# A fold that adds once instead of twice, and mirror values taken from the even part from step 18 on, with an earlier plan for the first two batches

## The chip, the cores and the metric

One core of one Trainium2 chip. The time is device time in microseconds (us). The kernel before took a median of 675.4 us (three runs, 675.08 to 675.92). The experiments were run in five rounds each (four to six runs of each), beside eleven runs of the kernel before on the same chip.

## The reference

```python
def _attn_ref(x):                       # x: 8 x 3008 x 256
    X = np.fft.fft(x, axis=1)
    X = np.fft.fft(X, axis=2)
    return X.real.astype(np.float32)

def _moe_ref(x, w_gate, w_val, w_out):  # 24064 x 256, d_ff 1536
    gate = np.maximum(x @ w_gate, 0.0)
    val = x @ w_val
    return (gate * val @ w_out).astype(np.float32)
```

A real 2-D Fourier transform of every batch, then a gated FFN on its rows. Inputs and output are float32.

## The kernel before

The transform over s (3008 = 94 x 32) is done in two stages on TensorE; the one over d (256) is folded into the FFN weights. Because the input is real, output row s and the mirror row S-s come from the same two products: P (even) and Q (odd). So only half the rows are transformed, and each FFN step makes two tiles of h: one for the rows (gate G, value V) and one for the mirror rows (gate G - 2Q-part, value V - 2Q-part).

The work is 8 batches x 3 blocks x 12 slices of d_ff = 288 steps. A step does five or six matmuls of 512 (or 480) columns and eight of 256 columns for the output. Meanwhile GpSimd (called POOL in the profile) folds the x of a later batch: it adds and subtracts mirror rows, so that the transform over s needs half the rows.

The fold, in chunks of three rows (`XC = 3`):

```python
def fold(b, eng):
    xl, xh, eo = xt[b]
    for lo in range(1, J - 1, XC):
        ...
        yield eng.tensor_tensor(c1, x1, rev, op=ALU.subtract)     # 768 elements
        yield eng.tensor_tensor(x1, x1, rev, op=ALU.add)          # 768 elements
        yield eng.tensor_tensor(e1[:, :, H + 1:D], c1[:, :, 1:H], ..., op=ALU.subtract)   # 381
        eng.tensor_copy(...)                                      # 6
        yield eng.tensor_tensor(e1[:, :, 1:H], x1[:, :, 1:H], ..., op=ALU.add)            # 381
    ...
```

The mirror value is made in one of two ways. In an unsplit step TensorE adds a third matmul to V and VectorE multiplies. In a split step VectorE makes E, the even part (V after its first matmul plus the "nb" row), then 2E - V, and POOL multiplies; one matmul is saved:

```python
def split(t):
    return NBLK * NF + 8 <= t < len(steps) and t % 3 != 2        # from step 44

def mirror_value(t):
    if split(t):
        nc.vector.scalar_tensor_tensor(E, E, 2.0, V, op0=ALU.mult, op1=ALU.subtract)
        mirror_h(t, nc.gpsimd, e["E"])
    else:
        nc.tensor.matmul(V, lhsT=wm[1]..., rhs=pq..., start=False, stop=True, ...)
        mirror_h(t, nc.vector, e["V"])
```

`nb` is one row of 512 numbers, spread over all partitions by way of DRAM. It is made at the end of stage 2 by two transfers, the second of which waits for the first:

```python
nc.sync.dma_start(out=row, in_=pq[0:1, 1, :])                                # Nd <- pq
nc.sync.dma_start(out=nbt[b, blk][:], in_=view(row, 0, [[0, 128], [1, 512]]))  # nb <- Nd
```

`gm` is the mirror gate after ReLU, in SBUF. "Rotate" is a small matmul that mends one column of the shuffled data before stage 2 reads it; VectorE casts its result back.

A table says at which step of batch b the parts for the next batches are placed: load of x (b+2), start of its fold, stage 1 (b+1), shuffle through DRAM, rotate, and six stage-2 pieces.

```python
plan = {0: (28, 34, (14, 16, 18, 19, 21, 23, 24, 25), 26, 33, (33, 34, 36, 38, 40, 42)),
        1: (12, 19, range(11, 19), 19, 26, (26, 27, 29, 31, 33, 35)),
        2: (7, 13, range(6, 14), 14, 22, (23, 25, 27, 29, 31, 33))}     # batches 2 to 7
```

`gm` and `E` are SBUF tiles with four buffers each (`ep = ...(name="ep", bufs=4, ...)`), V has three banks of PSUM.

## Time and profile before

| | before |
|---|---|
| median time | 675.4 us |
| TensorE (PE) busy | 643.4 us, 96% |
| VectorE (DVE), ScalarE (ACT), POOL busy | 74%, 64%, 64% |
| share of PE in the chain that ended last | 94% |
| steps 18 to 35 / batch 1 / each later batch | 42.24 / 79.42 / 76.33 us |

The last row is worked out from the timeline: a step is taken to begin where its second gate matmul begins, and the stretches are differences of such starts.

The page of the kernel before: busy time by engine, the chain that ended last by engine, and three groups of the fold (busy us, mean ns of one | idle before).

```profile
span 673.5 us, 12515 instructions
...
PE 643.4 (96%) x4218; PEld 419.9 (62%) x4297; DVE 500.8 (74%) x800; ACT 428.9 (64%) x811; POOL 428.5 (64%) x590
...
PE 94%; DMA 2%; DVE 2%; issue 1%; ACT 1%; SPq 0%; DVEq 0%; ACTq 0%
...
L99 POOL TENSOR_TENSOR xc<-xl,xh 94x768 f32<-94x768 f32 x35 | 63.6, 1817 | 39.6 <-DMA xl<-in_x_dram 24.8
L100 POOL TENSOR_TENSOR xl<-xl,xh 94x768 f32<-94x768 f32 x35 | 63.5, 1814 | 1.2
...
L104 POOL TENSOR_TENSOR eo<-xl 94x381 bf16<-94x381 f32 x35 | 34.8, 995 | 0.0
```

The fold is a large part of POOL's time, but the chain runs through PE. What is worth something is what shortens PE's stream or fills its gaps. The gaps are in the table of waits of PE (us in total, times, longest):

```profile
PE ps_169 L158 <- ACT w_98 L277: 12.0, 1, 12.0
PE ps_1264 L203 <- DVE t_1073 L192: 1.4, 1, 1.4
...
PE ps_2153 L203 <- DVE t_1949 L192: 1.1, 1, 1.1
```

The first is start-up. The two others are stage 2 of batches 1 and 2, which waits for the rotate result. The timeline of the kernel before (start us, us taken, engine, line, operation; in brackets the idle time before it and what ended it) shows how:

```profile
115.30 0.18 PE L191 MATMUL psr<-t_1073,rot 128*128 128x12 bf16 x1
...
115.50 0.65 DVE L475 TENSOR_TENSOR h<-gm,V 128x480 bf16<-128x480 f32 x1 [1.25 <-PE psr L191]
116.07 0.68 DVE L463 TENSOR_TENSOR h<-gs,V 128x512 bf16<-128x512 f32 x1
116.67 0.20 DVE L192 CAST t_1073<-psr 128x12 bf16<-128x12 f32 x1
116.93 0.38 PE L203 MATMUL ps_1264<-m_100,t_1073 128*128 128x128 bf16 x4 [1.44 <-DVE t_1073 L192]
```

The rotate matmul is at 115.30, its cast stands in VectorE's order behind two multiplies, and stage 2 stands right behind the rotate in PE's order (step 33 for both in the plan). So PE stands still for 1.44 us.

### The profile page before, as it was taken

The numbers are of one execution on the slowest core, as the hardware profiler recorded it, in microseconds if no ns is written. First come the engines' busy times: TensorE is split into PE (matmuls) and PEld (weight loads), VectorE is DVE, ScalarE is ACT, GpSimd is POOL, SyncE is SP. The second block draws the span as 40 slices with busy tenths as digits, with TensorE's granted clock in tenths as the row PEclk, the third lists the DMA queues.
The fourth block names the chain that finished last, engine by engine and source line by source line (L and its number), as shares of the span: only waits on it lengthen the run. The fifth ranks groups of instructions, "written<-read, shape, count | busy, mean of one in ns | idle before, by whom it ended". The sixth has DMA issues, their size and how long they took to land.

```text
span 673.5 us, 12515 instructions
## 1 busy us (share of the span) xinstructions
PE 643.4 (96%) x4218; PEld 419.9 (62%) x4297; DVE 500.8 (74%) x800; ACT 428.9 (64%) x811; POOL 428.5 (64%) x590
## 2 busy tenths in 40 slices
PE   2899999999999999999999999999999999999996
PEld 1444665666666666666666666666666666666665
DVE  8446555567787787887888888878878788888881
ACT  5455665667566757676666767676676766656562
POOL 1218910994999499946997399946997344344341
PEclk9999999999999999999999999999999999999999
DMA  9693138229413932277112931268211231211113
GB/s 240 209 224 47 43 97 236 63 52 216 147 48 90 231 97 57 60 158 212 47 45 66 228 119 41 77 142 212 57 46 51 69 107 39 79 33 46 46 33 92
DMA packets 31844, 70.75 MB, mean 105 GB/s; under 512 B 4410, under 2 KB 21426, under 8 KB 29394
## 3 DMA queue, kind: packets, MB, share of 16 engines
q1 hardware_dynamic: 29444, 58.16, 31.9%
q0 software_dynamic: 2336, 11.80, 8.7%
q8 instruction: 33, 0.54, 0.4%
q14 instruction: 31, 0.25, 0.1%
HBM read 39.77 MB, written 30.96 MB: 105 GB/s over the span
## 4 chain that ended last, share of the span: by engine, by line
PE 94%; DMA 2%; DVE 2%; issue 1%; ACT 1%; SPq 0%; DVEq 0%; ACTq 0%
PE po L505 38%; PE G L438 10%; PE V L461 9%; PE G L449 9%; PE V L459 8%; PE G L437 8%; PE V L487 4%; PE psw L251 4%; DMA xh<-in_x_dram 2%; DVE h L463 1%; DVE eo L130 0%; DVE E L469 0%; SPq L119 0%; ACT gm L452 0%; ACT os L508 0%
## 5 line engine op out<-in xcount | busy, mean ns | idle before, releaser
L505 PE MATMUL po<-wo,h 128*128 128x256 bf16 x2304 | 323.3, 273 | 1.8
L475 POOL TENSOR_TENSOR h<-gm,E 128x480 bf16<-128x480 f32 (+1 forms) x162 | 199.1, 1229 | 147.9 <-DVE E L483 147.2
L505 PEld LDWEIGHTS <-h 128*128 128x128 bf16 x2304 | 222.8, 98 | 82.7 <-issue 7.6
L452 ACT ACTIVATE gm<-G 128x480 f32<-128x480 f32 (+1 forms) x288 | 167.4, 581 | 134.0 <-PE G L449 130.4
L463 DVE TENSOR_TENSOR h<-gs,V 128x512 bf16<-128x512 f32 x288 | 190.6, 684 | 47.5 <-PE V L461 40.4
L439 ACT ACTIVATE gs<-G 128x512 f32<-128x512 f32 x288 | 171.8, 597 | 2.2 <-POOL si L399 2.2
L475 DVE TENSOR_TENSOR h<-gm,V 128x480 bf16<-128x480 f32 (+1 forms) x126 | 83.7, 664 | 87.8 <-ACT gm L452 63.2
L469 DVE SCALAR_TENSOR_TENSOR E<-nb,af,V 128x480 f32<-128x480 bf16 (+1 forms) x162 | 117.2, 723 | 7.4 <-PE V L459 5.9
L438 PE MATMUL G<-pq,ws_105 128*128 128x512 bf16 x287 | 108.8, 379 | 2.0
L449 PE MATMUL G<-pq,wm_107 128*128 128x480 bf16 (+1 forms) x288 | 106.7, 371 | 1.0 <-ACT gs L439 1.0
L483 DVE SCALAR_TENSOR_TENSOR E<-E,V 128x480 f32<-128x480 f32 (+1 forms) x162 | 106.6, 658 | 0.0
L461 PE MATMUL V<-pq,ws_106 128*128 128x512 bf16 x272 | 103.0, 379 | 0.2
L459 PE MATMUL V<-pq,wc_104 128*128 128x512 bf16 x265 | 100.5, 379 | 0.0
L508 ACT COPY os<-po 128x512 f32<-128x512 f32 x96 | 56.2, 585 | 68.3 <-PE po L505 68.3
L437 PE MATMUL G<-pq,wc_103 128*128 128x512 bf16 x249 | 94.4, 379 | 1.0 <-ACT pq L206 1.0
L99 POOL TENSOR_TENSOR xc<-xl,xh 94x768 f32<-94x768 f32 x35 | 63.6, 1817 | 39.6 <-DMA xl<-in_x_dram 24.8
L100 POOL TENSOR_TENSOR xl<-xl,xh 94x768 f32<-94x768 f32 x35 | 63.5, 1814 | 1.2
L461 PEld LDWEIGHTS <-ws_106 128*128 128x128 bf16 x288 | 28.2, 98 | 33.8 <-DVE ws_106 L256 0.4
L438 PEld LDWEIGHTS <-ws_105 128*128 128x128 bf16 x288 | 28.2, 98 | 32.4 <-issue 1.1
L487 PE MATMUL V<-pq,wm_108 128*128 128x480 bf16 (+1 forms) x126 | 46.6, 370 | 0.2
L459 PEld LDWEIGHTS <-wc_104 128*128 128x128 bf16 x288 | 28.2, 98 | 17.5 <-issue 1.3
L104 POOL TENSOR_TENSOR eo<-xl 94x381 bf16<-94x381 f32 x35 | 34.8, 995 | 0.0
(362 smaller groups left out, 401.5 us busy)
## 6 DMA issues: line engine op xcount, KB each, us to landing
out_dram<-os SPq DMA_DIRECT2D x176, 128.0 KB
xl<-in_x_dram SPq DMA_DIRECT2D x7, 1360.0 KB
nb<-Nd SPq DMA_DIRECT2D x24, 128.0 KB
xl<-in_x_dram SPq DMA_DIRECT2D x7, 238.0 KB
xl<-in_x_dram SPq DMA_DIRECT2D x2, 768.0 KB
xh<-in_x_dram SPq DMA_DIRECT2D x2, 768.0 KB
wst<-in_moe_w_gate_dram SPq DMA_DIRECT2D x6, 256.0 KB
wst<-in_moe_w_val_dram SPq DMA_DIRECT2D x6, 256.0 KB
```

Of the source, the lines that this page charges most:

```text
L437: nc.tensor.matmul(e["G"][:], lhsT=wc[0][:, fs], rhs=pq[:, 0, :], start=True, stop=False)
L438: nc.tensor.matmul(e["G"][:], lhsT=ws[0][:, fs], rhs=pq[:, 1, :], start=False, stop=True)
L439: nc.scalar.activation(e["gs"][:], e["G"][:], ACTF.Relu)
L449: nc.tensor.matmul(e["G"][:, cols], lhsT=wm[0][:, f * 128:(f + 1) * 128], rhs=pqt[b, blk][:, 1, cols], start=False, stop=True, skip_group_ ...
L452: nc.scalar.activation(e["gm"][:, cols], e["G"][:, cols], ACTF.Relu)
L459: nc.tensor.matmul(e["V"][:], lhsT=wc[1][:, fs], rhs=pq[:, 0, :], start=True, stop=split(t))
L461: nc.tensor.matmul(e["V"][:], lhsT=ws[1][:, fs], rhs=pq[:, 1, :], start=False, stop=True, skip_group_check=split(t))
L463: nc.vector.tensor_tensor(e["h"][:, 0, :], e["gs"][:], e["V"][:], op=ALU.mult)
L469: nc.vector.scalar_tensor_tensor(e["E"][:, cols], nbt[b, blk][:, cols], af[:, f:f + 1], e["V"][:, cols], op0=ALU.mult, op1=ALU.add)
L475: eng.tensor_tensor(free(e["h"][:], 512 + cols.start + NB - 1, [NB, (cols.stop - cols.start) // NB], [-1, NB]), e["gm"][:, cols].rearrange ...
L483: nc.vector.scalar_tensor_tensor(e["E"][:, cols], e["E"][:, cols], 2.0, e["V"][:, cols], op0=ALU.mult, op1=ALU.subtract)
L505: nc.tensor.matmul(po[:, s % 2, :], lhsT=ht[t - f + ff]["h"][:, sg, g * 128:(g + 1) * 128], rhs=wo[:, ff, :], start=(ff == 0), stop=(ff == ...
```

## The change

The intent: since x is folded over s and then over d, one add over s with d reversed, u[d] = x[s,d] + x[S-s,D-d], is enough; its even and odd parts over d are both results. That is one large operation on POOL per chunk instead of two, and fewer pieces (17 instead of 22 per fold). The room on POOL is used to split from step 18 on instead of 44, and batches 0 and 1 get an earlier plan.

```diff
     def fold(b, eng):
         xl, xh, eo = xt[b]
         for lo in range(1, J - 1, XC):
-            ...
-            yield eng.tensor_tensor(c1, x1, rev, op=ALU.subtract)
-            yield eng.tensor_tensor(x1, x1, rev, op=ALU.add)
-            yield eng.tensor_tensor(e1[:, :, H + 1:D], c1[:, :, 1:H], free(c1, D - 1, [D, n], [-1, H - 1]),
-                                    op=ALU.subtract)
-            eng.tensor_copy(free(e1, 0, [D, n], [H, 2]), free(x1, 0, [D, n], [H, 2]))
-            yield eng.tensor_tensor(e1[:, :, 1:H], x1[:, :, 1:H], free(x1, D - 1, [D, n], [-1, H - 1]), op=ALU.add)
+            n = min(XC, J - 1 - lo)
+            x1, e1, m = xl[0:NA, lo:lo + n, :], eo[:, lo:lo + n, :], (NB // 2 - lo) * D
+            eng.tensor_tensor(free(e1, 0, [D, n], [H, 2]), free(x1, 0, [D, n], [H, 2]),
+                              free(xh[0:NA], m, [-D, n], [H, 2]), op=ALU.add)
+            yield eng.tensor_tensor(x1[:, :, 1:D], x1[:, :, 1:D], free(xh[0:NA], m + D - 1, [-D, n], [-1, D - 1]),
+                                    op=ALU.add)
+            for op, o in ((ALU.add, 1), (ALU.subtract, H + 1)):
+                yield eng.tensor_tensor(e1[:, :, o:o + H - 1], x1[:, :, 1:H], free(x1, D - 1, [D, n], [-1, H - 1]),
+                                        op=op)
@@
-        return NBLK * NF + 8 <= t < len(steps) and t % 3 != 2
+        return 18 <= t < len(steps) and t % 3 != 2
@@
-    plan = {0: (28, 34, (14, 16, 18, 19, 21, 23, 24, 25), 26, 33, (33, 34, 36, 38, 40, 42)),
-            1: (12, 19, range(11, 19), 19, 26, (26, 27, 29, 31, 33, 35)),
-            2: (7, 13, range(6, 14), 14, 22, (23, 25, 27, 29, 31, 33))}
+    plan = {0: (18, 24, (16, 17, 18, 19, 20, 21, 22, 23), 24, 31, (32, 33, 35, 37, 39, 41)),
+            1: (7, 13, range(6, 14), 14, 22, (23, 25, 27, 29, 31, 33))}
@@
-        for k in range(2 if t < NBLK * NF + 8 else 1):
-            while folds and next(folds[0], folds) is folds:
-                folds.pop(0)
+        while folds and next(folds[0], folds) is folds:
+            folds.pop(0)
```

The last hunk is how fast a fold is handed to POOL: two pieces a step up to step 43 before, one piece a step now.

More of the change, by code (lines that the diff above doesn't have):

```diff
@@ L58 @@
     xp = ctx.enter_context(tc.tile_pool(name="xp", bufs=1, space=SB))
-    xcp = ctx.enter_context(tc.tile_pool(name="xcp", bufs=2, space=SB))
     tp = ctx.enter_context(tc.tile_pool(name="tp", bufs=2, space=SB))
@@ L93, in fold @@
         for lo in range(1, J - 1, XC):
-            hi = min(lo + XC, J - 1)
-            n = hi - lo
-            x1, e1 = xl[0:NA, lo:hi, :], eo[:, lo:hi, :]
-            rev = free(xh[0:NA], (NB // 2 - lo) * D, [-D, n], [1, D])
-            c1 = xcp.tile([NA, XC, D], F32, tag="xc", name="xc")[:, 0:n, :]
-            yield eng.tensor_tensor(c1, x1, rev, op=ALU.subtract)
-            yield eng.tensor_tensor(x1, x1, rev, op=ALU.add)
-            yield eng.tensor_tensor(e1[:, :, H + 1:D], c1[:, :, 1:H], free(c1, D - 1, [D, n], [-1, H - 1]),
-                                    op=ALU.subtract)
-            eng.tensor_copy(free(e1, 0, [D, n], [H, 2]), free(x1, 0, [D, n], [H, 2]))
-            yield eng.tensor_tensor(e1[:, :, 1:H], x1[:, :, 1:H], free(x1, D - 1, [D, n], [-1, H - 1]), op=ALU.add)
+            n = min(XC, J - 1 - lo)
[7 more added lines that the diff above has]
+                                        op=op)
         ends = free(xl[0:NA], 0, [(J - 1) * D, 2], [H, 2])
@@ L535 @@
     at(9, nyquist)
-    plan = {0: (28, 34, (14, 16, 18, 19, 21, 23, 24, 25), 26, 33, (33, 34, 36, 38, 40, 42)),
-            1: (12, 19, range(11, 19), 19, 26, (26, 27, 29, 31, 33, 35)),
-            2: (7, 13, range(6, 14), 14, 22, (23, 25, 27, 29, 31, 33))}
+    plan = {0: (18, 24, (16, 17, 18, 19, 20, 21, 22, 23), 24, 31, (32, 33, 35, 37, 39, 41)),
+            1: (7, 13, range(6, 14), 14, 22, (23, 25, 27, 29, 31, 33))}
     for b in range(B):
         t0 = b * NBLK * NF
-        tl, tf, t1, tsh, tr, t2 = plan[min(b, 2)]
+        tl, tf, t1, tsh, tr, t2 = plan[min(b, 1)]
         if b + 2 < B:
```

## The prediction

> **What bounds it now.** TensorE: the page has PE busy 643 of 673.5 us (96%), VectorE 74%, GpSimd (POOL) and ScalarE 64%; the chain of waits runs 94% through PE. The Trainium skill ("Perfetto Trace Analysis", Identifying the Most-Contended Engine) warns that matmul busy time is no measure of headroom, so I took PE's cadence from the timeline: 512 columns start every 0.213 us, back to back in nearly all steps. After start-up (34.8 us) the table of PE waits holds 1.44 and 1.11 us for the DVE cast of the "rotate" result (batches 1 and 2), and about 1 us once more. Where POOL is busy 33.98 of 34 us (238 to 272, 476 to 510), PE is still busy 33.79: POOL is not on the chain.
>
> **What the change does.**
> 1. Fold on POOL: a chunk becomes a 6-element add (0.21 us), one 765-element op (about 1.85, from the 768-element ones at 1.81) and two of 381 (0.99 each): 4.0 us, not 5.8; over 35 chunks 62 us less. Worth nothing by itself; it makes room for 2. Fold 1 should end near 73 us, not 82.
> 2. Split from step 18, not 44: 18 more steps get the mirror value from VectorE and POOL. Removed: 18 mirror matmuls, 0.20 to 0.21 us of PE cadence each. Added: 18 pairs of DVE ops (0.71 + 0.65) less 18 DVE multiplies (0.66), and 18 POOL multiplies (1.21 to 1.27). The skill's "GPSIMD Engine Reference" says GpSimd can't access PSUM; the trace agrees so far as every POOL multiply reads E, not V.
> 3. Plan: in batches 0 and 1 rotate and the first stage 2 now stand a step apart instead of in one step. From batch 2 on they already do, with no PE wait: the two waits go.
>
> **Sum, from step cadence** (starts of the second gate matmul).
> - Steps 18 to 35 take 42.24 us. In steady batches a triple of steps, two of them split, takes about 6.18 (512 columns) or 6.08 (480) without stage 1 or 2. After: 2 x 6.18 + 4 x 6.08, nine stage 1/2 groups at 0.215 and the rotate, about 38.75. Gain 3.5.
> - Batch 1 takes 79.42; a steady batch 76.33, plus three left-over stage-2 groups: 76.98. Gain 2.4.
> - Batches 2 to 7, start-up, tail: 0; only POOL gets slack.
>
> Total 5.9 us, all on the critical path: about 3.5 from matmuls left out, 2.4 from waits. Less 0.3 for small new stalls.
>
> **Prediction: 669.7 us, 8 in 10 between 668.2 and 672.0.** Faster by over 2%: 0.02; within 2%: 0.97; slower: 0.01.
>
> **What will show it.** 36 PE instructions fewer; mirror value matmul x108; POOL multiplies x180; POOL busy about 428 - 62 + 22 = 388 us; DVE up by about 12; no PE wait for the rotate cast; batch 1 near 77.0; batches 2 to 7 still 76.3 each; PE 95% of the chain.
>
> **What would make it wrong.** (a) Load x of batch 2 starts at step 18, its fold at step 24, some 13.4 us later; that load took 13.6 us before. If it lands late, in-order POOL holds the mirror multiplies behind the fold; gm has four buffers, so over about 4 us of lag reaches PE. (b) Splits at step 36 need the nb row made at step 33: two dependent transfers in some 6 us; a late one stalls VectorE, then PE through V's three banks. (c) The 765-element op with a fully reversed operand could be slower. (d) Eight stage 1 evacuations, one per step, load ScalarE to 2.0 of 2.2 us. Each could cost 1 to 2 us.

## The result, and the profile after

The changed kernel took a median of 669.73 us (four runs, 668.58 to 670.72) against 675.66. The ratio is 0.9912, 95% interval 0.9892 to 0.9932; repeated in five rounds it was 0.9901 (0.9888 to 0.9915). Ratios are the mean time of one kernel's runs over that of the other's runs of the same rounds, so they are not quite the ratio of the medians that are quoted.

The page of the changed kernel (its line numbers are two to four lower than before; L98 and L101 are the new fold, L473 the multiply on POOL):

```profile
span 668.5 us, 12493 instructions
...
PE 640.5 (96%) x4201; PEld 417.9 (63%) x4279; DVE 513.0 (77%) x818; ACT 428.7 (64%) x811; POOL 391.1 (59%) x573
...
PE 91%; issue 3%; DMA 2%; DVE 2%; POOL 1%; ACT 0%; SPq 0%; DVEq 0%; POOLq 0%
...
L473 POOL TENSOR_TENSOR h<-gm,E 128x480 bf16<-128x480 f32 (+1 forms) x180 | 221.0, 1228 | 208.4 <-DVE E L481 202.8
...
L101 POOL TENSOR_TENSOR eo<-xl 94x381 bf16<-94x381 f32 x70 | 68.7, 994 | 0.4
L98 POOL TENSOR_TENSOR xl<-xl,xh 94x765 f32<-94x765 f32 x35 | 63.2, 1805 | 2.7
```

There are 18 weight loads fewer (PEld x4297 to x4279), 18 VectorE instructions and 18 POOL multiplies more (x162 to x180), and POOL is busy 37 us less. The table of waits of PE no longer holds the two rotate waits; start-up and two short waits in the first steps (1.9 us; 1.0 in one before) are what is left of any size:

```profile
PE ps L156 <- ACT w L275: 12.1, 1, 12.1
PE G L447 <- ACT gs L437: 1.9, 2, 1.0
```

The timeline of the changed kernel at the same place shows the step put between rotate and stage 2 (the plan says 31 and 32):

```profile
109.86 0.18 PE L189 MATMUL psr<-t,rot 128*128 128x12 bf16 x1
...
110.13 0.69 DVE L461 TENSOR_TENSOR h<-gs,V 128x512 bf16<-128x512 f32 x1 [0.54 <-PE psr L189]
110.74 0.20 DVE L190 CAST t<-psr 128x12 bf16<-128x12 f32 x1
...
112.26 0.39 PE L201 MATMUL ps<-m,t 128*128 128x128 bf16 x4
```

The cast is done at 110.94, stage 2 comes at 112.26 without a wait.

Where the time went, by stretches of steps (starts of the second gate matmul, us, profiled runs):

| steps | before | after | difference |
|---|---|---|---|
| 0 to 11 | 31.98 | 32.87 | +0.89 |
| 12 to 17 | 13.72 | 13.73 | 0 |
| 18 to 35 | 42.24 | 38.59 | -3.65 |
| 36 to 71 (batch 1) | 79.42 | 77.28 | -2.14 |
| each of batches 2 to 6 | 76.33 | 76.33 | 0 |
| 252 to 286 | 71.40 | 71.23 | -0.17 |

The stretches are not the causes. Steps 18 to 35 hold only 12 of the 18 new splits, and they hold the first rotate wait (step 33); batch 1 holds the other six splits (steps 36 to 43) and the second wait. The profile of e6 below, the changed kernel without the early split, separates the two: it took 40.86 us in steps 18 to 35 and 27.30 in steps 36 to 47, where the changed kernel took 38.59 and 26.14. So the split is worth 2.27 us in the first stretch and 1.16 in the second, 3.43 in all, and 1.38 of the 3.65 us are the plan's.

The +0.89 in the first steps is not counted to the change: steps 0 to 11 took between 31.7 and 33.9 us in the fourteen profiles, with the new fold and without it. In the changed kernel's profile a copy on POOL (the one that releases the buffer of a weight load) waited 13.5 us for a weight load (12.2 before), and ScalarE's first gate output waited for that copy, 3.1 us instead of 2.2. This scatter is why a single run doesn't decide 1%.

### The profile page after: what moved, and what is told of

It is laid out like the page before. It is cut to its first block, busy times and chain, and to the rows that moved or that the text cites. A ratio compares the mean times of both kernels' runs of the same rounds, so it can differ in the third digit from the quotient of the medians.

```text
span 668.5 us, 12493 instructions
## 1 busy us (share of the span) xinstructions
PE 640.5 (96%) x4201; PEld 417.9 (63%) x4279; DVE 513.0 (77%) x818; ACT 428.7 (64%) x811; POOL 391.1 (59%) x573
## 4 chain that ended last, share of the span: by engine, by line
PE 91%; issue 3%; DMA 2%; DVE 2%; POOL 1%; ACT 0%; SPq 0%; DVEq 0%; POOLq 0%
PE po L503 38%; PE G L436 10%; PE V L459 10%; PE V L457 9%; PE G L447 9%; PE G L435 7%; PE V L485 3%; DMA xh<-in_x_dram 2%; PE psw L249 2%; PE ps L159 2%; PE ps L201 2%; DVE E L467 1%; DVE eo L128 0%; PE ps L164 0%; DVE h L461 0%
## 5 line engine op out<-in xcount | busy, mean ns | idle before, releaser
L473 POOL TENSOR_TENSOR h<-gm,E 128x480 bf16<-128x480 f32 (+1 forms) x180 | 221.0, 1228 | 208.4 <-DVE E L481 202.8
L473 DVE TENSOR_TENSOR h<-gm,V 128x480 bf16<-128x480 f32 (+1 forms) x108 | 71.9, 665 | 62.8 <-ACT gm L450 57.1
L436 PE MATMUL G<-pq,ws 128*128 128x512 bf16 x282 | 106.9, 379 | 2.6
L447 PE MATMUL G<-pq,wm 128*128 128x480 bf16 (+1 forms) x288 | 106.7, 370 | 1.9 <-ACT gs L437 1.9
L459 PE MATMUL V<-pq,ws 128*128 128x512 bf16 x280 | 106.0, 378 | 0.5
L457 PE MATMUL V<-pq,wc 128*128 128x512 bf16 x273 | 103.5, 379 | 0.0
L435 PE MATMUL G<-pq,wc 128*128 128x512 bf16 x239 | 90.6, 379 | 1.0 <-ACT pq L204 1.0
L101 POOL TENSOR_TENSOR eo<-xl 94x381 bf16<-94x381 f32 x70 | 68.7, 994 | 0.4
L98 POOL TENSOR_TENSOR xl<-xl,xh 94x765 f32<-94x765 f32 x35 | 63.2, 1805 | 2.7
L459 PEld LDWEIGHTS <-ws 128*128 128x128 bf16 x288 | 28.2, 98 | 34.0 <-DVE ws L254 0.4
L436 PEld LDWEIGHTS <-ws 128*128 128x128 bf16 x288 | 28.2, 98 | 32.4 <-issue 1.1
L169 ACT CAST t<-ps 96x512 bf16<-96x512 f32 x64 | 37.4, 584 | 6.3 <-PE ps L157 3.2
L485 PE MATMUL V<-pq,wm 128*128 128x480 bf16 (+1 forms) x108 | 40.0, 370 | 0.2
```

The lines of the kernel that those rows point to most:

```text
L435: nc.tensor.matmul(e["G"][:], lhsT=wc[0][:, fs], rhs=pq[:, 0, :], start=True, stop=False)
L436: nc.tensor.matmul(e["G"][:], lhsT=ws[0][:, fs], rhs=pq[:, 1, :], start=False, stop=True)
L447: nc.tensor.matmul(e["G"][:, cols], lhsT=wm[0][:, f * 128:(f + 1) * 128], rhs=pqt[b, blk][:, 1, cols], start=False, stop=True, skip_group_ ...
L457: nc.tensor.matmul(e["V"][:], lhsT=wc[1][:, fs], rhs=pq[:, 0, :], start=True, stop=split(t))
L459: nc.tensor.matmul(e["V"][:], lhsT=ws[1][:, fs], rhs=pq[:, 1, :], start=False, stop=True, skip_group_check=split(t))
L473: eng.tensor_tensor(free(e["h"][:], 512 + cols.start + NB - 1, [NB, (cols.stop - cols.start) // NB], [-1, NB]), e["gm"][:, cols].rearrange ...
```

## The experiments

The question was whether the sum of the prediction is right for the right reasons: is the gain the 18 matmuls and the two waits; is the fold worth nothing by itself, yet needed; and is the plan only about rotate? Each part was put into the kernel before alone, then each was taken out of the changed kernel alone. "Before" is the median of the kernel before in the same rounds: 676.15 us for e1 to e4, 675.84 for e5 to e8, 676.04 for e9 to e12; these three groups ran on three chips, so comparisons across groups, as of e7 with e9 and e10, lean on these medians agreeing to 0.3 us. All kernels gave correct results.

### e1: the fold alone

The kernel before with the new fold, handed over one piece a step.

```diff
-            yield eng.tensor_tensor(c1, x1, rev, op=ALU.subtract)
-            yield eng.tensor_tensor(x1, x1, rev, op=ALU.add)
+            (the new fold, as in the change)
-        for k in range(2 if t < NBLK * NF + 8 else 1):
```

> Only the cheaper fold (and its one piece per step) in the kernel before; split from step 44 and the old plan stay. Theory A (TensorE cadence and the rotate waits are all of the gain, the fold only makes room): POOL busy falls by about 60 us, from 428 to about 368, the time stays within 0.6 us of before, and the two rotate waits (1.4 and 1.1 us) stay in the table of PE waits. Rival B (POOL was holding the kernel back, its relief pays): 2 to 6 us faster.

676.09 us, ratio 0.9998 (0.9985 to 1.001). POOL busy fell from 428.5 to 370.1 us, and both rotate waits stayed (2.0 us in two). So 58 us of POOL are worth nothing by themselves, and rival B is out.

### e2: the plan alone

```diff
-    plan = {0: (28, 34, ...), 1: (12, 19, ...), 2: (7, 13, ...)}
+    plan = {0: (18, 24, ...), 1: (7, 13, ...)}
```

> Only the new plan (when batch 2 is loaded, when stage 1, shuffle, rotate and stage 2 run in batches 0 and 1); fold and split as before. Theory A: the two rotate waits go, 2.0 to 2.6 us faster, nothing else. Rival C (the whole gain is the matmuls left out by the split): within 0.6 us of before.

673.44 us, ratio 0.9959 (0.9947 to 0.9971): 2.7 us, a little over the expected range, and the rotate waits are gone.

### e3: rotate one step earlier, and nothing else

```diff
-    plan = {0: (28, 34, (14, 16, ...), 26, 33, (33, 34, ...)),
-            1: (12, 19, range(11, 19), 19, 26, (26, 27, ...)),
+    plan = {0: (28, 34, (14, 16, ...), 26, 32, (33, 34, ...)),
+            1: (12, 19, range(11, 19), 19, 25, (26, 27, ...)),
```

> The kernel before with two numbers changed: rotate in batch 0 at step 32 instead of 33 and in batch 1 at 25 instead of 26, so that it stands one step ahead of its first stage 2. Theory A: the same 2.0 to 2.6 us as the whole new plan gives, and no PE wait for the rotate cast. Rival D (the plan's gain comes from the earlier load and stage 1, not from rotate): under 0.6 us.

673.16 us, ratio 0.9953 (0.994 to 0.9965): 3.0 us by medians, as much as the whole plan within the intervals. In its profile steps 30 to 35 took 13.32 us instead of 14.92, steps 60 to 71 took 26.18 instead of 26.88; no wait for the rotate cast is left. Without the split, all that the plan gains is gained by two numbers in it.

### e4: the split alone

```diff
-        return NBLK * NF + 8 <= t < len(steps) and t % 3 != 2
+        return 18 <= t < len(steps) and t % 3 != 2
```

> Only the split from step 18; old fold (two pieces a step up to step 43), old plan. In steps 34 to 43 POOL is given about 30 us of fold and 9 us of mirror multiplies and memsets in some 21 us of TensorE time. Theory A (the fold makes room): the mirror multiplies fall behind, ScalarE waits for gm buffers, TensorE stalls by some 8 to 13 us there, so 4 to 10 us SLOWER than before although 18 matmuls are gone. Rival E (the cheaper fold was not needed): 3.0 to 3.7 us faster, as the sum of cadences says.

686.37 us, ratio 1.0146 (1.013 to 1.0162): 10 us slower, at the upper end of what was expected. Steps 18 to 35 gained 2.7 us (39.53 instead of 42.24), then steps 36 to 47 took 38.17 instead of 26.48. The timeline of e4 there:

```profile
138.67 1.82 POOL L99 TENSOR_TENSOR xc<-xl,xh 94x768 f32<-94x768 f32 x1
140.57 1.82 POOL L100 TENSOR_TENSOR xl<-xl,xh 94x768 f32<-94x768 f32 x1
...
144.50 1.20 POOL L475 TENSOR_TENSOR h<-gm,E 128x480 bf16<-128x480 f32 x1
...
145.73 0.57 ACT L452 ACTIVATE gm<-G 128x480 f32<-128x480 f32 x1 [3.09 <-POOL h L475]
...
146.84 0.36 PE L449 MATMUL G<-pq,wm 128*128 128x480 bf16 x1 [1.40 <-ACT gs L439]
```

This is the expected chain: a mirror multiply stands behind pieces of the fold, ScalarE can't write gm until that multiply has read its buffer, and PE waits for ScalarE. But the table of waits also held one that was not in the theory: PE waited 3.9 us once for an E of VectorE, and VectorE waited 4.2 us for nb.

### e5: the changed kernel without the new fold

```diff
+            (the old fold, as before)
-        while folds and next(folds[0], folds) is folds:
-            folds.pop(0)
+        for k in range(2 if t < 43 and t % 4 == 0 else 1):
+            while folds and next(folds[0], folds) is folds:
+                folds.pop(0)
```

> The changed kernel with the old fold put back. Its 22 pieces have to be done before the next load of x (step 43), as the new fold's 17 are, so up to step 42 every fourth step takes two pieces. Theory A (the fold only makes room, but the room is needed): from step 24 to 41 POOL has about 30 us of fold and 17 us of multiplies and memsets in some 38 us of TensorE time; about 5 us of lag were borne without a stall in the kernel before, so TensorE stalls by about 4 us: about 673.5, between 671.5 and 676. Rival E (the cheaper fold was not needed for the gain): as the changed kernel, 669 to 670.5.

678.91 us, ratio 1.0052 (1.0039 to 1.0064): 9 us slower than the changed kernel, twice what was expected, and slower than the kernel before. ScalarE waited 23.6 us for POOL's multiplies before it could write gm (3.8 in the changed kernel). The windows of e5 from 120 us on (busy us of each engine in 8 us; PE first, then weight loads, VectorE, ScalarE, POOL, then granted clock and DMA):

```profile
120.00:128.00 8.00, 7.43 (x56) 4.83 (x54) 5.83 (x10) 4.83 (x9) 8.00 (x11) 1.00 0.32 83
128.00:136.00 8.00, 6.96 (x47) 4.18 (x45) 5.31 (x9) 4.11 (x8) 8.00 (x11) 1.00 0.06 19
136.00:144.00 8.00, 6.96 (x47) 4.38 (x46) 4.88 (x9) 5.18 (x10) 8.00 (x13) 1.00 0.21 68
```

POOL is busy throughout, 8.00 of 8 us; PE is not. The same window of the changed kernel has PE back at its full 7.9 while POOL comes to rest:

```profile
128.00:136.00 8.00, 7.95 (x58) 5.41 (x57) 6.08 (x11) 5.93 (x12) 7.44 (x15) 1.00 0.06 19
136.00:144.00 8.00, 7.90 (x55) 5.51 (x56) 6.30 (x10) 5.85 (x12) 2.60 (x5) 1.00 0.95 248
```

The author reports that the old fold can't simply be handed over more slowly: the split alone with one piece a step and the old plan is said to deadlock when it is built, since 22 pieces from step 34 are not done when x is loaded again at step 48 (the arithmetic holds; the failed build is not on record). So at the rate of hand-over tried here the cheaper fold is needed: it turns a loss of 3 us into a gain of 6. Other rates for the old fold were not tried. How much lag POOL may have before PE feels it was estimated too high here.

### e6: the changed kernel without the early split

```diff
-        return 18 <= t < len(steps) and t % 3 != 2
+        return NBLK * NF + 8 <= t < len(steps) and t % 3 != 2
```

> The changed kernel with the split put back to step 44. Theory A: fold and plan together give what the plan alone gave, so 2.0 to 3.0 us faster than before, about 673.3; the 18 mirror matmuls of steps 18 to 43 are the rest. Rival B (POOL relief counts together with the plan): below 672.

673.41 us, ratio 0.9963 (0.995 to 0.9976): 2.4 us, what the plan gives alone. The split in steps 18 to 43 is the other 3.5 us, and by stretches 3.43, as said above.

### e7: the changed kernel without the new plan

```diff
-    plan = {0: (18, 24, ...), 1: (7, 13, ...)}
+    plan = {0: (28, 34, ...), 1: (12, 19, ...), 2: (7, 13, ...)}
```

> The changed kernel with the old plan (fold of batch 2 from step 34, rotate in the same step as its first stage 2). Theory A: fold and split together give 3.0 to 3.8 us, about 672.4; the two rotate waits of 1.1 to 1.5 us are in the table of PE waits; no stall from POOL, though the split alone cost 10 us, since the new fold asks 20 us of POOL in 17 steps and not 30 in 11. Rival: if the split alone was slow for another reason than POOL's load (VectorE, or early nb), this is slow too, over 676.

679.91 us, ratio 1.0057 (1.004 to 1.0075). This is a miss by 7.5 us: the kernel is slower than before, though POOL has the cheap fold. The expectation had named this outcome as the sign of another reason. The cause is at step 37. From the timeline of e7 (SPq is the queue that issues the transfers):

```profile
103.89 1.11 SPq L81 DMA_DIRECT2D xl<-in_x_dram  x2
103.97 1.02 POOL L84 DMA_INDIRECT xh<-in_x_dram,ix  x1 [0.17 <-issue]
...
119.14 0.23 SPq L210 DMA_DIRECT2D Nd<-pq  x1
125.74 0.34 SPq L211 DMA_DIRECT2D nb<-Nd  x1
...
128.81 0.71 DVE L467 SCALAR_TENSOR_TENSOR E<-nb,af,V 128x480 f32<-128x480 bf16 x1 [5.44 <-DMA nb<-Nd]
...
129.58 0.58 PE L459 MATMUL V<-pq,ws 128*128 128x512 bf16 x1 [5.21 <-DVE E L467]
```

The row of 1 KB was sent at 119.14, and the transfer that depends on it could be issued only at 125.74, 6.6 us later; in the kernel before the same pair was 1.15 us apart:

```profile
92.83 1.01 POOL L85 DMA_INDIRECT xh<-in_x_dram,ix  x1 [0.64 <-PE V L487]
...
105.62 1.11 SPq L82 DMA_DIRECT2D xl<-in_x_dram  x2
...
120.32 0.23 SPq L212 DMA_DIRECT2D Nd<-pq  x1
121.47 0.34 SPq L213 DMA_DIRECT2D nb<-Nd  x1
```

The load of x for batch 2 has two halves, xl issued by SPq and xh issued by POOL. In e7 they were issued together, at 103.89 and 103.97, and POOL's fold waited for xh until 125.12. In the kernel before POOL issued its half already at 92.83, 12.8 us ahead of the other, and the fold began at 119.18. That is an effect of the early split which the prediction did not have: the three runs with the old plan and the late split (before, e1, e3) issue xh at 92.8 to 94.0, and the three with the old plan and the early split (e4, e7, e8) at 102.8 to 104.0, where POOL's multiplies stand in front of it. So the split does two things to nb. Without it nobody needs this nb before step 44, and with it step 36 does; and it makes the load end later, so that the row is late. VectorE did nothing else for 5.4 us, and PE stood with it.

The wait cost more than its 5.2 us, since the clock fell. Windows of e7 around it (third number from the end of a line is the granted clock):

```profile
124.00:129.50 5.50, 0.37 (x2) 0.09 (x1) 0.69 (x1) 1.04 (x2) 4.30 (x7) 0.76 0.49 169
129.50:133.00 3.50, 3.42 (x13) 1.80 (x13) 1.99 (x4) 0.00 (x0) 0.96 (x3) 0.50 0.03 11
133.00:137.00 4.00, 4.00 (x29) 2.54 (x28) 2.31 (x4) 3.25 (x6) 3.92 (x5) 0.92 0.02 6
```

The clock record of the trace has 0.50 from 126.83 to 133.65. So 4.1 us of work after the gap ran at half clock, and 512 columns took 0.42 us to issue instead of 0.21. The Trainium skill ("TensorE: Matmul & The Clock Gate", Part 1: The HAM clock gate) says that after at least one idle window of about 3.4 us the array runs at half clock until it has been busy for about as long. The return agrees with this trace: PE was busy from 130.24 to 133.65, 3.41 us, before it. The fall came sooner: at 126.83 PE had been idle for 2.5 us, since 124.37. Steps 37 and 38 together took 11.67 us, against 4.38 in the changed kernel: 7.3 us more, of which 5.2 are the wait and about 2.0 the clock (an estimate, half of the 4.1 us).

### e8: the split alone, with six buffers instead of four for gm and E

```diff
-    ep = ctx.enter_context(tc.tile_pool(name="ep", bufs=4, space=SB))
+    ep = ctx.enter_context(tc.tile_pool(name="ep", bufs=6, space=SB))
```

> The split alone (10 us slower than before) with six buffers instead of four for gm and E. Theory A (the multiplies queue behind the fold on POOL, and the wait reaches TensorE through the gm and E buffers): two buffers more bear two steps more of lag, about 4.3 us, so 681 to 683 instead of 686.4, and steps 36 to 47 take about 34 us instead of 38.2. Rival F (the wait is for something else: the nb row, the h buffers, VectorE's own load): unchanged within 1 us.

684.76 us, ratio 1.0131 (1.0115 to 1.0148): 1.6 us better than e4, less than the 3.4 to 5.4 expected. In steps 36 to 47 the buffers did more than expected (32.25 us instead of 38.17), but steps 48 to 71 gave 3.9 us back (58.21 instead of 54.27). So the gm and E buffers do pass POOL's lag on to PE, and rival F is not all of it; but more buffers mostly put the wait off while POOL is overloaded. The wait for nb, 5.1 us at PE, stands in this profile too: F was right about part of e4's loss.

### e9: e7 with the load of x for batch 2 ten steps earlier

```diff
-    plan = {0: (28, 34, (14, 16, ...), 26, 33, (33, 34, ...)),
+    plan = {0: (18, 34, (14, 16, ...), 26, 33, (33, 34, ...)),
```

> The kernel without the new plan (679.9 us, when 672.4 was expected) with one number changed: x of batch 2 is loaded from step 18 instead of 28; fold, stage 1, rotate and stage 2 stay where the old plan has them. In its profile TensorE waited 5.2 us at step 37 for an E of VectorE, which waited 5.4 us for the nb row; the write of that row was issued at 119.1 us and landed only at 125.7, while the load of x was still under way. Theory G (the split needs nb at step 36, and the load of x holds the two small transfers up): the wait goes, 672 to 674 us; what is left to the changed kernel is the two rotate waits. Rival H (stage 2 one step later is the cause, two dependent transfers don't fit into two steps): 677 or more.

672.54 us, ratio 0.9949 (0.9937 to 0.9961). One number is worth 7.4 us. Rival H is out: stage 2 stands where it stood. In the timeline of e9 the first transfer now has the way free:

```profile
85.19 0.89 SPq L81 DMA_DIRECT2D xl<-in_x_dram  x2
...
117.98 0.23 SPq L210 DMA_DIRECT2D Nd<-pq  x1
119.12 0.34 SPq L211 DMA_DIRECT2D nb<-Nd  x1
```

1.14 us lie between the two, and no wait of VectorE for nb is left. What remains to the changed kernel, 2.7 us, is the rotate: PE waits for it twice in this profile, 1.7 us together. No run takes the delay of so small a transfer apart, but the packet records in the traces show what stood before it. In e7 the row's one packet of 1024 bytes started at 125.04. The packets of xl, issued before it on the same SPq queue, ended at 122.65, those of xh on POOL's queue at 124.40, and those of the output stores, issued at 108.41 on SPq, at 125.20. In the kernel before these ends were at 118.56, 101.71 and 119.82, and the row's packet started at 121.02, 0.7 us after its issue. So the row stood behind older transfers of its own queue; xl took 15.4 us from its first packet to the end of its last with xh beside it (e7), and 9.6 us without (before). The Trainium skill ("DMA: Bandwidth & Descriptors", Issuing engines are not separate DMA queues) says that transfers of all issuing engines run on the same 16 DMA engines and interleave; the 6.6 us of e7, with both halves under way, and the 1.14 us of e9, with none, fit that.

### e10, e11, e12: the changed kernel again, and a denser split

e11 uses the room that is left: three of four steps split from step 48 on, and the later folds spread out.

```diff
-        return 18 <= t < len(steps) and t % 3 != 2
+        return 18 <= t < len(steps) and (t % 3 != 2 if t < 48 else t % 4 != 3)
@@
-        while folds and next(folds[0], folds) is folds:
+        while (t < 49 or t % 3) and folds and next(folds[0], folds) is folds:
```

e12 has only the first of these two hunks. e10 is the changed kernel, unaltered.

> The changed kernel unaltered, for a narrow interval beside the others: 669 to 671 us, ratio 0.990 to 0.993.

> The changed kernel with three of four steps split from step 48 on instead of two of three (20 more mirror matmuls left out), and the folds from batch 3 on spread to two pieces in three steps (17 pieces in 25 steps, before the next load). Theory A (TensorE cadence decides as long as POOL and VectorE keep up; VectorE would be at about 7.5 of 8.0 us in four steps, POOL at about 1.9 of 2.0 us a step): 20 x 0.17 = 3.4 us faster than the changed kernel, 665.5 to 667.5. Rival I (three splits in a row exhaust V's three banks or VectorE): no gain or slower.

> As the one before, but the folds keep one piece a step. POOL is then asked for about 2.36 us a step during a fold, against some 2.03 of TensorE, over 17 steps: 5.6 us of lag, a little over the 4 to 5 that were borne. Theory A: up to 1.5 us of stall in each of batches 2 to 5, so 667 to 672, slower than the spread version. Rival J (the lag that is borne is larger): the same as the spread version.

| | median us | ratio to before (95%) |
|---|---|---|
| e10 changed kernel | 669.88 | 0.9901 (0.9888 to 0.9915) |
| e11 denser, folds spread | 663.24 | 0.9816 (0.9803 to 0.9828) |
| e12 denser, one piece a step | 664.91 | 0.9829 (0.9813 to 0.9845) |

e11 beats both kernels, and by twice what was expected: 6.6 us, which is 0.33 for each of its 20 extra splits, not 0.17. In the stretch without folds, steps 252 to 286, the changed kernel took 71.23 us and e11 69.92: 1.31 us for three extra splits, 0.44 each, of which the matmul left out is 0.20 to 0.21. The starts of PE's matmuls in the profiles of e10 and e11 account for the rest. In the changed kernel two split steps follow each other in every three, and in the second of them the second V matmul starts 0.06 to 0.12 us late, 0.05 us after VectorE has finished the E that reads the same bank of V. These waits are too short for the table of waits. In steps 252 to 275 they sum to 0.68 us in e10 and to 0.15 in e11; with two matmuls fewer (0.42 us) that is the whole difference, 49.02 against 48.08 us. So in the changed kernel a little of PE's time is a wait for VectorE, and the denser split removes most of it. Why E comes in time there was not followed up.

e12 can't be told from e11 by its interval. In its profile, which is of the slowest of its five runs (669.11 us), batches 3 to 6 take the same time as in e11 to 0.01 us, and steps 48 to 107 lost 2.9 us together. So in the later batches one piece a step was borne: rival J is right there, and a stall in every batch, as theory A had it, did not come.

## Why the prediction was right or wrong

The time was right: 669.7 predicted, 669.73 measured, 669.88 again. By its points:

- **TensorE bounds the kernel, POOL isn't on the chain.** Right, shown by e1: 58 us less on POOL and no time gained.
- **Steps 18 to 35 at 38.75 us, batch 1 at 76.98, later batches at 76.3.** Right to 0.3: 38.59, 77.28 and 76.33.
- **"About 3.5 from matmuls left out, 2.4 from waits".** The sizes are right: 18 splits gave 3.5 us (e6), the plan without the split 2.7 (e2), rotate alone 3.0 (e3). But the way to them was wrong, and that they agree is luck. The 3.5 was worked out for steps 18 to 35, which hold 12 of the 18 splits and the first rotate wait; the 2.4 was worked out for batch 1, which holds the other six and the second wait. By e6, steps 18 to 35 gained 2.27 us from matmuls and 1.38 from the plan. The total is not touched by this, since the two stretches together hold all of both.
- **What the plan is for.** This step was incomplete. "Plan: in batches 0 and 1 rotate and the first stage 2 now stand a step apart" is what it does when the split is late. With the early split the plan is worth 10.0 us (e7 against e10), and 7.4 of them are the load of x, moved out of the way of the nb row (e9). The prediction had nb among the things that might go wrong, but took the earlier load only as a risk, not as the cure; and it did not see that the split itself delays POOL's half of the load.
- **The fold makes room.** Right in kind, shown by e5; the size of what happens without it, given as about 4 us when e5 was planned, was about 9.
- **Risk (a), a late load in front of the fold; (b), nb; (c), the reversed operand; (d), ScalarE.** None came in the changed kernel. The 765-element operation with d reversed took 1805 ns, the 768-element one before 1814 to 1817. (b) came as soon as the plan was taken away, and cost 7.4 us, not "1 to 2".
- **Signs.** POOL busy 391.1 us (388 predicted), DVE up by 12.2 (12), 180 multiplies on POOL, 18 weight loads fewer: right. Two signs were off: fold 1 ended at 75.4 us, not near 73 (it began at 53.4, not 52.0, and took 22), and PE is 91% of the chain, not 95%. Why the chain leaves PE a little more often was not followed up; PE's own table of waits doesn't show it.

The parts do not add up: alone they give 0.0, -2.7 and +10.2 us, together -6.2. Fold and plan each remove one of the two things that break the early split, POOL's overload and the late nb.

Left open: how much lag of POOL TensorE can bear (about 5 us was assumed; e5 lost more than that allows, e12's later batches lost nothing); and how e4's loss divides between the fold and nb. Against e9, which has neither the overload nor the late row, e4 took 5.8 us more in steps 37 and 38 (10.08 against 4.32), where the wait for nb is, and 7.1 more in steps 39 to 47 (25.95 against 18.85); but the late row also shifts POOL's work, so this divides the loss by place and not by cause.

## What to carry to other kernels

Where one engine is the bound, count its stream in cadence, step by step, and price a change by steps left out and waits removed; relief of another engine is room to move work into, not time. Before work is moved earlier, ask for each of its inputs when it arrives, small transfers too: here a transfer of 1 KB that stood behind a load of some 3 MB came 5.4 us late. And ask what the moved work itself pushes back: here it was the issue of that load. Take the parts of a change out one at a time from the finished kernel as well as putting them in alone: only the first showed what the plan was for.

## What the Trainium skill lacked or had wrong

- "DMA: Bandwidth & Descriptors" has no figure for what a small transfer pays beside a large load. Here the pair of dependent transfers was 6.6 us apart while both halves of a load of x were under way (e7) and 1.14 us without it (e9).
- "GPSIMD Engine Reference" doesn't say what a reversed operand (negative step) costs. Here nothing that can be measured: 1805 ns for 765 elements with d reversed, 1814 to 1817 ns for 768 with only the rows reversed.
- "TensorE: Matmul & The Clock Gate", Part 1: The HAM clock gate, lets the clock fall after an idle window of about 3.4 us. Here it fell when PE had been idle for 2.5 us (e7, at 126.83), 2.3 us (e4, at 151.28) and 2.0 us (e8, at 159.05). In the 3.41 us before each of these falls PE was busy for 0.96, 1.14 and 1.44 us. After 3.41 us with 2.01 us busy (e4, from 144.46) and with 1.71 us busy (e8, from 121.50) it did not fall.
